# Attention and MoE in one kernel: eight more dummy matmuls in the head, and a kv product moved across a slab boundary

## The chip, the core and the metric

The kernel runs on one core of a Trainium2 chip. The core has five engines that run side by side and wait for each other by semaphores: PE (TensorE, matrix products into the eight banks of PSUM), DVE (VectorE), ACT (ScalarE), POOL (GpSimd) and SP (SyncE, which here only issues DMAs). The metric is the device time of one execution in microseconds (us). Three timed runs of the kernel before gave 280.95, 281.73 and 280.97 us; the median is 280.97 us.

## The reference

Eight batches of linear attention (8 heads, 576 positions, head size 64) feed a two-layer network with a swish that has one beta for each hidden unit. In short:

```python
q_s = softmax(q, axis=-1)                      # over the 64 of a head
k_s = softmax(k, axis=2)                       # over the 576 positions
kv  = einsum('bhsd,bhse->bhde', k_s, v)        # 64 x 64 for each head
x   = einsum('bhsd,bhde->bhse', q_s, kv)       # to (4608, 512)
h   = x @ w_in                                 # (4608, 2048)
g   = h * sigmoid(beta * h)
out = g @ w_out                                # (4608, 512), f32
```

## The kernel before, in words

**Slabs.** The 4608 rows are nine slabs of 512. Slab b (0 to 7) holds the first 512 positions of batch b; slab 8 holds the last 64 positions of all eight. For each slab PE runs two passes. Pass 1 (`pass1_mm`, line 638) makes 16 hidden tiles f of 128 units, each from four products over m (the four head pairs, 128 columns each), `WIN` by `XT`; after the fourth, ACT applies Silu from the PSUM bank into `GT[:, f]` (L646). Pass 2 (`pass2_group`, L727) multiplies `GT` by `WOUT` into four row groups u, each over 16 f; a copy (`o2_evac`, L700) takes each from its bank to `O2S`, and `store` writes it out. The two passes are 64 products of 512 columns each, 0.216 us apart.

**Attention.** For a batch, `exp_q` and `exp_kc` on ACT make the exponentials EQ and EK, `norm_main` on DVE and POOL divides EQ by its row sums, `cast_v` turns V into bf16 with a column of ones behind it. `kv_prods` multiplies EK by V on PE, `kv_evac` divides by the last column on DVE (reciprocal RC, L442, and product KVC, L444). `out_prods` multiplies the transposed EQ (`QT`) by KVC, and `out_evac` (L456) copies the results from PSUM to `XT`: odd head pairs on ACT, even ones on DVE. `kv_half` and `out_half` do two of the four pairs.

**Head.** Batch 0 has its own order, written out by hand (L603 to L634): long f32 dummy products first, then for each head pair four transposes of EQ (`t_steps`), a kv product (`kv_tiles`, 18 products of 65 columns), an out product (`out_now`), and between them four dummies `warm(1, bank)`, one bf16 product of zeros with 512 columns each, read by nobody. Slab 0's pass 1 follows.

**From slab 0 to slab 1.** During slab 0's pass 2, a list `todo` (L754) places batch 1's attention at counted products (`tick`): transposes at 104 and 109, the first kv half at 115, the first out half at 122, then `evacs` at 124.5 (row group u0 by DVE out of bank 3, u1 by ACT out of bank 4, then a dummy activation that brings Silu's table back), and the second kv half at 127, one product before the pass ends. After it come the copy of u2 (bank 5, ACT) and slab 1's opening tiles: for a set of f, all products of m = 0, then all of m = 1 and so on (`by_m`, L655), so that the first rows need only the first XT pairs. `FIRST = (16, 5)` says how many tiles: 16 in slab 0, 5 in slab 1. Between them lie the second out half (banks 7 and 0) and the copy of u3 (bank 6, DVE).

**Banks.** `hbank` (L652) gives pass 1's tile its PSUM bank from a table: slab 1's f0 to f7 take banks 1, 3, 2, 4, 5, 6, 0, 7, and f8 and on take 2, 0, 1 in turn. A product that starts a tile waits until the engine that last read its bank is done.

**What sets the order.** Each engine runs its instructions in the order in which `add` (L57) was called for it. `Program.plan` turns the declared reads, writes and banks into semaphore waits; nothing is reordered. DMAs are issued by SP in the order of the calls as well.

Of the kernel before, what the change touches and what calls it, by code (L numbers as in the profile page):

```python
# [163 lines left out]
def bass_efficient_attn_shen__then__act_swish_beta_kernel(  # L164
# [12 lines left out]
    with ExitStack() as es:  # L177
# [113 lines left out]
        for hp in range(NHP):  # L291
            eng = ACTE if hp % 2 else SP
# [39 lines left out]
        def norm_main(b, hp0, n, eng=DVE):  # L332
            i = b % 2
            a = bass.AP(EQ[i], hp0 * 512, [[2048, 128], [64, 8 * n], [1, 64]])
            s_ = bass.AP(QS[i], hp0 * 8, [[32, 128], [1, 8 * n]])
            v_ = bass.AP(QI[i], hp0 * 8, [[32, 128], [1, 8 * n]])
            vb = bass.AP(QI[i], hp0 * 8, [[32, 128], [1, 8 * n], [0, 64]])
            ks = [("eq", i, hp) for hp in range(hp0, hp0 + n)]
            add(DVE, lambda e: e.tensor_reduce(s_, a, AX.X, ALU.add), r=ks, w=[("qs", i, hp0)])  # L339
            add(DVE, lambda e: e.reciprocal(v_, s_), r=[("qs", i, hp0)], w=[("qi", i, hp0)])  # L340
            add(eng, lambda e: e.tensor_tensor(a, a, vb, ALU.mult), r=ks + [("qi", i, hp0)],  # L341
                w=ks)
# [113 lines left out]
        def out_evac(b, bks, hps=range(NHP)):  # L456
            i = b % 2
            for hp in hps:
                eng, bk = (ACTE if hp % 2 else DVE), bks[hp]
                add(eng, lambda e, eng=eng, bk=bk, hp=hp: (  # L460
                    e.copy if eng == ACTE else e.tensor_copy)(XT[i][:, hp, :], PS[bk][:, :]),
                    r=[("ps", bk)], w=[("xt", i, hp)], bank=[bk])
# [19 lines left out]
        def kv_half(b, bks, a):  # L482
            kv_prods(b, bks, (a,))
            kv_evac(b, bks, (a,))

        def out_half(b, bks, a):
            out_prods(b, bks, (a,))
            out_evac(b, bks, (a, a + 1))
# [53 lines left out]
        def go(steps):  # L542
            for s in steps:
                s()
# [67 lines left out]
        turn_beta()  # L612
        norm_main(0, 2, 1, POOL)
        norm_main(0, 3, 1, POOL)
        go(t_steps(0, (1,), (4,)))
        kv_tiles(0, 7)
        warm(1, 0)
        cast_v(0, 2)
        cast_v(0, 3)
        for m in range(1, NM):  # L620
            cast_win(0, m, POOL)
        cast_win(1, 0, POOL)
        go(t_steps(0, (2,), (5,)))
        warm(1, 0)
        kv_tiles(1, 1)
        out_now(0, 0, 0, ACTE)
        go(t_steps(0, (3,), (6,)))
        warm(1, 3)
        kv_tiles(2, 7)
        out_now(0, 1, 5, ACTE)  # L630
        cast_win(0, 0, DVE)
        warm(1, 3)
        out_now(0, 2, 0, ACTE)
        kv_tiles(3, 1)  # L634

# [1 line left out]

        def pass1_mm(t, f, m, bk):
            x = XT8 if t == 8 else XT[t % 2]
            rd = [("xt8", 0)] + [("xt8", p_, y) for p_ in range(1, 4) for y in range(2)] if t == 8 else [("xt", t % 2, m)]  # L640
            n = 2 if f < 8 else 4
            l = bass.AP(WIN, m * DFF + 128 * (f // n * n) + f % n, [[NM * DFF, 128], [n, 128]])
            mm(PS[bk][:, :], l, x[:, m, :], m == 0, m == NM - 1,
               r=rd + [("win", f // 4, m)], w=[("ps", bk)], bk=bk)
            if m == NM - 1:
                add(ACTE, lambda e: e.activation(GT[:, f, :], PS[bk][:, :], ACT.Silu,  # L646
                                                 scale=BETA[:, f:f + 1]),
                    r=[("ps", bk), "beta"], w=[("gt", f)], bank=[bk])
# [15 lines left out]
                pass1_mm(t, f, m, bk)  # L664
                tick()

        FIRST = (16, 5)
        at = by_m(0, 0, 4)
        at(0)
        out_now(0, 3, 7, DVE)  # L670
# [74 lines left out]
        for t in range(NSLAB):  # L745
            todo = []
            if t == 0:
                def evacs():
                    o2_evac(0, 0, 3, DVE)
                    o2_evac(0, 1, 4, ACTE)  # L750
                    add(ACTE, lambda e: e.activation(DUMMY[:, 2:3], WARM[:, 0:1], ACT.Silu),
                        r=["warm"], w=["dummy"])

                todo = [(104, lambda: go(t_steps(1, (0, 1), (1,), ACTE))),  # L754
                        (104.1, lambda: cast_v(1, 0, ACTE)),
                        (109, lambda: go(t_steps(1, (2, 3), (2,), ACTE))),
                        (109.1, lambda: (scale_wout(14, 2), exp_kc(1, 2), exp_kc(1, 3))),
                        (115, lambda: kv_half(1, (7, 0), 0)),
                        (122, lambda: out_half(1, (1, 2), 0)), (124.5, evacs),
                        (127, lambda: kv_half(1, (7, 0), 2))]  # L760
            elif t == 1:
                todo = [(103, lambda: (kv_prods(2, (1, 2), (0, 2)), kv_evac(2, (1, 2)))),
                        (118, lambda: block(2))]
            elif t < 7:
                todo = [(104, lambda: block(t + 1))]
            todo = sorted(todo, key=lambda x: -x[0])
            slot = [0]

            def tick():
                slot[0] += 1  # L770
                while todo and todo[-1][0] <= slot[0]:
                    todo.pop()[1]()

            if 2 <= t < 7:
                if t < 5:
                    load(t + 2 if t == 2 else t + 3)
                for hp in (0, 2):
                    norm_main(t + 1, hp, 2)
                    t_dma(t + 1, hp, 2)
                if t in (2, 3, 4, 6):  # L780
                    norm_rem(t // 2 if t != 3 else 0)
                    tr_dma(t // 2 if t != 3 else 0)
                if t == 2:
                    load(5)
            elif t == 1:
                for hp in range(NHP):
                    cast_v(2, hp)
            if t < 2:
                slot[0] = NM * FIRST[t]
            for f in range(FIRST[t] if t < 2 else 0, NF):  # L790
                pass1_tile(t, f, tick)
            if t == 0:
                load(2)
                scale_wout(0)
                scale_wout(4)
                exp_q(1, (0,))
                norm_main(1, 0, 1)
                scale_wout(8)
                exp_q(1, (1, 3, 2))
                norm_main(1, 1, 1, POOL)  # L800
                norm_main(1, 3, 1, POOL)
                norm_main(1, 2, 1)
                exp_kc(1, 0, 2)
                scale_wout(12, 2)
                for hp in range(1, NHP):
                    cast_v(1, hp)
                pass2_group(0, (0, 1, 2, 3), (3, 4, 5, 6), tick)
                while todo:
                    todo.pop()[1]()
                at = by_m(1, 0, FIRST[1])  # L810
                o2_evac(0, 2, 5, ACTE)
                at(0, 0, 3)
                at(1, 0, 3)
                out_half(1, (7, 7, 7, 0), 2)
                o2_evac(0, 3, 6, DVE)
                at(0, 3)
                at(1, 3)
                at(2)
                at(3)
                store(0)  # L820
                load(3)
                load_qrem(0)
                continue
            nb = [t + 2] if t + 2 < B else []
            if t == 1:
                nb = [2, 3]
            late = []
            for b in nb:
                if t == 1 and b == 2:
                    exp_q(2)  # L830
                    for hp in range(2):
                        norm_main(2, hp, 1, POOL)
                    t_dma(2, 0, 2)
                for hp in (0, 2):
                    exp_kc(b, hp, 2)
                if b > 2:
                    late.append(b)
                if b > 3:
                    for hp in range(NHP):
                        cast_v(b, hp)  # L840
            for b in late:
                exp_q(b)
                if b % 2 == 1:
                    exp_qr(b // 2)
                if b == 3:
                    exp_qr(0)
            for u in range(4):
                if (t, u) == (8, 3):
                    last_tile(u, ((0, 384), (384, 512)), (OB[orot[0] % 2], MB[0]))
                    continue  # L850
                pass2_group(t, (u,), (OB[orot[0] % 2],), tick)
                orot[0] += 1
                if t == 1 and u == 0:
                    for hp in range(2, 4):
                        norm_main(2, hp, 1, POOL if hp == 2 else DVE)
                    t_dma(2, 2, 2)
                    for hp in range(NHP):
                        cast_v(3, hp)
            while todo:
                todo.pop()[1]()  # L860
            if t < 8:
                store(t)
# [30 lines left out]
```

## Time and profile before

| what | value |
| --- | --- |
| median of three runs | 280.97 us |
| profiled execution | 281.7 us |
| its span, first to last instruction | 279.9 us |
| busy share PE / DVE / ACT / POOL | 97% / 37% / 60% / 12% |
| chain that ended last, PE's share | 94% |
| slab 0's first product starts at | 16.05 us |
| second kv half of batch 1 on PE | 45.86 us |
| its last inputs are cast by | 44.20 us (EK, ACT), 44.99 us (V, POOL) |

How to read it: the page gives one execution, all times from the first instruction. A group row names the source line, the engine, the operation, what is written from what, the shapes, and how often. Most of PE's rows have L371 or L373, the helper `mm`, so they are told apart by their tiles: `PS<-WARM` is a dummy, `PS<-IDB,EQ` a transpose, `PS<-VB,EK` a kv product, `PS<-QT,KVC` an out product, `PS<-XT,WIN` pass 1 and `PS<-WOUT,GT` pass 2. Busy time counts an instruction until its result is written; a matmul of 512 columns lasts 0.38 us by its row though the next starts 0.216 us after it. PEclk is the share of full TensorE clock that was granted. In brackets stands the engine's idle time before a row and what ended it. Some matmul records are missing from the trace: after kv products a hole of 0.16 us marked "issue" is one of them.

### The profile page before, as it was taken

To read this page: it belongs to the slowest core of one execution; us is meant where nothing else is said; L and a number is where in the kernel's file an instruction comes from. 1 tells how busy PE (TensorE), PEld (TensorE's weight loads), DVE (VectorE), ACT (ScalarE), POOL (GpSimd) and SP (SyncE) were. 2 spreads that over 40 slices of the span, in tenths; PEclk is the share of its full clock that TensorE was granted. 3 is DMA by queue.
4 is the path that set the end of the run, shared out by engine and by line. 5 is a ranking of instruction groups with operands and counts; after the bars stand their busy time and mean duration, and the time that the engine had idled before them with its cause. 6 is when DMAs were issued, how large, how long until landed. Compare 5 with 4: busy or idle time off the path is not lost.

```text
span 279.9 us, 4581 instructions
## 1 busy us (share of the span) xinstructions
PE 270.9 (97%) x1892; PEld 131.8 (47%) x1922; DVE 103.0 (37%) x206; ACT 166.6 (60%) x240; POOL 33.2 (12%) x50
## 2 busy tenths in 40 slices
PE   7799999999999999999999999999999999999995
PEld 2545454454445454545454544444444444444443
DVE  3663695007590157305640463035603300110012
ACT  4657777789767835794479537853751276017500
POOL 2630041306100305030002100000000000000000
PEclk9689999999999999999999999999999999999999
DMA  7999999997279998970499134001600120011022
GB/s 226 387 388 401 388 390 376 360 384 119 42 239 389 204 374 229 387 171 2 144 356 235 40 129 96 2 4 75 169 0 2 49 101 2 0 74 76 2 75 75
DMA packets 42173, 50.12 MB, mean 179 GB/s; under 512 B 21028, under 2 KB 29476, under 8 KB 41000
## 3 DMA queue, kind: packets, MB, share of 16 engines
q1 hardware_dynamic: 41168, 48.77, 54.3%
q10 hardware_dynamic: 984, 1.06, 1.2%
q8 instruction: 15, 0.25, 0.4%
q14 instruction: 6, 0.05, 0.0%
HBM read 36.71 MB, written 9.44 MB: 165 GB/s over the span
## 4 chain that ended last, share of the span: by engine, by line
PE 94%; DMA 2%; issue 1%; ACTq 0%; ACT 0%; DVE 0%
PE PS L373 93%; DMA QF<-in_q_dram 2%; PE PS L371 1%; ACTq L299 0%; ACT EK L323 0%; ACT VB L358 0%; DVE O2S L722 0%; ACT EQ L315 0%; ACTq L147 0%
## 5 line engine op out<-in xcount | busy, mean ns | idle before, releaser
L646 ACT ACTIVATE GT<-PS,BETA 128x512 bf16<-128x512 f32 x144 | 96.9, 689 | 61.3 <-PE PS L373 61.3
L373 PE MATMUL PS<-WOUT,GT 128*128 128x512 bf16 (+2 forms) x573 | 125.0, 373 | 1.8 <-issue 1.3
L373 PE MATMUL PS<-XT,WIN 128*128 128x512 bf16 x566 | 125.8, 379 | 0.7 <-issue 0.2
L373 PEld LDWEIGHTS PS<-XT,WIN 128*128 128x128 bf16 x576 | 60.4, 106 | 63.6 <-issue 0.5
L373 PEld LDWEIGHTS PS<-WOUT,GT 128*128 128x128 bf16 x592 | 56.5, 98 | 65.8 <-issue 1.1
L701 DVE COPY O2S<-PS 128x512 f32<-128x512 f32 x33 | 22.7, 688 | 124.1 <-PE PS L373 124.1
L358 POOL CAST VB<-VF 128x576 bf16<-128x576 f32 x29 | 20.8, 718 | 84.8 <-DMA VF<-in_v_dram 83.2
L339 DVE TENSOR_REDUCE QS<-EQ 128x8 f32<-128x512 bf16 (+1 forms) x22 | 20.1, 913 | 19.6 <-ACT EQ L315 19.6
L460 ACT CAST XT<-PS 128x512 bf16<-128x512 f32 x14 | 7.6, 589 | 23.9 <-PE PS L373 23.9
L315 ACT ACTIVATE EQ<-QF 128x512 bf16<-128x512 f32 x32 | 17.7, 617 | 3.5 <-DMA QF<-in_q_dram 3.5
L323 ACT ACTIVATE EK<-KF 128x1152 bf16<-128x1152 f32 (+1 forms) x19 | 18.4, 1005 | 1.7 <-DMA KF<-in_k_dram 1.6
L341 DVE TENSOR_TENSOR EQ<-EQ,QI 128x1024 bf16<-128x1024 bf16 (+1 forms) x14 | 16.3, 1164 | 0.5
L460 DVE CAST XT<-PS 128x512 bf16<-128x512 f32 x14 | 9.1, 688 | 13.4 <-PE PS L373 13.4
L341 POOL TENSOR_TENSOR EQ<-EQ,QI 128x512 bf16<-128x512 bf16 x8 | 8.3, 1043 | 35.4 <-DVE QI L340 35.0
L373 PEld LDWEIGHTS PS<-VB,EK 64*64 64x64 bf16 x576 | 7.4, 112 | 5.3 <-issue 2.5
L373 PE MATMUL PS<-VB,EK 64*64 64x65 bf16 x576 | 8.9, 200 | 1.0 <-ACT VB L358 0.6
L373 PE MATMUL PS<-QT,KVC 64*64 64x512 bf16 x64 | 6.9, 405 | 0.0
L646 ACT ACT_TABLE_LOAD x5 | 6.4, 1283 | 0.1
L373 PE MATMUL PS<-XT 128*128 128x512 f32 x6 | 5.0, 998 | 1.5 <-DVE XT L226 1.5
L340 DVE RECIPROCAL QI<-QS 128x8 f32<-128x8 f32 (+1 forms) x22 | 5.0, 226 | 0.8
L323 ACT ACT_TABLE_LOAD x4 | 5.1, 1283 | 0.1
L444 DVE TENSOR_TENSOR KVC<-PS,RC 128x128 bf16<-128x128 f32 (+1 forms) x16 | 4.4, 275 | 0.6
(51 smaller groups left out, 66.6 us busy)
## 6 DMA issues: line engine op xcount, KB each, us to landing
out_dram<-O2S SPq DMA_DIRECT2D x8, 1024.0 KB, 4.5
QF<-in_q_dram SPq DMA_DIRECT2D x30, 256.0 KB, 5.7
KF<-in_k_dram SPq DMA_DIRECT2D x6, 1152.0 KB, 8.0
VF<-in_v_dram SPq DMA_DIRECT2D x6, 1152.0 KB, 10.9
KF<-in_k_dram SPq DMA_DIRECT2D x8, 288.0 KB, 8.3
VF<-in_v_dram SPq DMA_DIRECT2D x8, 288.0 KB, 8.6
WST<-in_moe_w_in_dram SPq DMA_DIRECT2D x8, 256.0 KB, 7.6
O2S<-in_moe_w_in_dram SPq DMA_DIRECT2D x4, 512.0 KB, 11.8
```

The source lines that it names most:

```text
L315: add(ACTE, lambda e, o=o, a=a: e.activation(o, a, ACT.Exp), r=[("qf", i, hp, x) for x in ((2, 3) if hp % 2 else (hp // 2,))], w=[("eq", i ...
L323: add(ACTE, lambda e: e.activation(o, a, ACT.Exp), r=[("kf", i, h) for h in range(hp, hp + n)], w=[("ekc", i, h) for h in range(hp, hp + n)])
L339: add(DVE, lambda e: e.tensor_reduce(s_, a, AX.X, ALU.add), r=ks, w=[("qs", i, hp0)])
L340: add(DVE, lambda e: e.reciprocal(v_, s_), r=[("qs", i, hp0)], w=[("qi", i, hp0)])
L341: add(eng, lambda e: e.tensor_tensor(a, a, vb, ALU.mult), r=ks + [("qi", i, hp0)], w=ks)
L358: add(eng, lambda e: (e.copy if eng == ACTE else e.tensor_copy)(o, a), r=[("vf", i, hp), ("vone", i)], w=[("vb", i, hp, h) for h in ((0, 1 ...
L371: add(PE, lambda e: e.transpose(o, l, r_), r=r, w=w, bank=[bk])
L373: add(PE, lambda e: e.matmul(o, l, r_, start=start, stop=stop, tile_position=tp), r=r, w=w, bank=[bk])
L444: add(DVE, lambda e, o=o, p_=p_, vb=vb: e.tensor_tensor(o, p_, vb, ALU.mult), r=[("ps", bk)] + [("rc", i, hp) for hp in hps], w=[("kvc", k ...
L460: add(eng, lambda e, eng=eng, bk=bk, hp=hp: (e.copy if eng == ACTE else e.tensor_copy)(XT[i][:, hp, :], PS[bk][:, :]), r=[("ps", bk)], w=[ ...
L646: add(ACTE, lambda e: e.activation(GT[:, f, :], PS[bk][:, :], ACT.Silu, scale=BETA[:, f:f + 1]), r=[("ps", bk), "beta"], w=[("gt", f)], ba ...
L701: add(eng, lambda e: (e.copy if eng == ACTE else e.tensor_copy)(O2S[t % 2][:, u, :], PS[bk][:, :]), r=[("ps", bk)], w=[("o2", t % 2, u)], ...
```

## The change

Five edits. (1) The head gets eight more bf16 dummies (the change's own summary counts nine): two new ones ahead of pair 1's transposes, and 3, 2, 2, 3 where there was one each. (2) Batch 1's second kv half leaves the list at 127 and stands in slab 1, behind two products of the opening tiles; the copy of u3 (bank 6) follows it directly and no longer the second out half. (3) Slab 1 opens with six tiles, and is split behind two tiles and not three. (4) In batch 1, pairs 2 and 3 swap engines for their XT copies: pair 2 on ACT, pair 3 on DVE. (5) Slab 8's products name all eight copies into XT8 as their inputs. In the order of instructions the kernel has eight matmuls more and no other instruction more or less; on DVE the copy of u3 comes ahead of an XT copy; SP's order of DMAs is the same.

```diff
@@ out_evac
-                eng, bk = (ACTE if hp % 2 else DVE), bks[hp]
+                eng, bk = (ACTE if (hp % 2) != (b == 1 and hp > 1) else DVE), bks[hp]
@@ the head
         norm_main(0, 3, 1, POOL)
+        warm(2, 0)
         go(t_steps(0, (1,), (4,)))
         kv_tiles(0, 7)
-        warm(1, 0)
+        warm(3, 0)
         cast_v(0, 2)
...
         go(t_steps(0, (2,), (5,)))
-        warm(1, 0)
+        warm(2, 0)
         kv_tiles(1, 1)
         out_now(0, 0, 0, ACTE)
         go(t_steps(0, (3,), (6,)))
-        warm(1, 3)
+        warm(2, 3)
         kv_tiles(2, 7)
         out_now(0, 1, 5, ACTE)
         cast_win(0, 0, DVE)
-        warm(1, 3)
+        warm(3, 3)
         out_now(0, 2, 0, ACTE)
         kv_tiles(3, 1)
@@ pass1_mm
-            rd = [("xt8", 0)] + [("xt8", p_, y) for p_ in range(1, 4) for y in range(2)] if t == 8 else [("xt", t % 2, m)]
+            rd = ([("xt8", p_, y) for p_ in range(4) for y in range(2)] if t == 8
+                  else [("xt", t % 2, m)])
@@ opening tiles
-        FIRST = (16, 5)
+        FIRST = (16, 6)
@@ todo of slab 0
-                        (122, lambda: out_half(1, (1, 2), 0)), (124.5, evacs),
-                        (127, lambda: kv_half(1, (7, 0), 2))]
+                        (122, lambda: out_half(1, (1, 2), 0)), (124.5, evacs)]
@@ the end of slab 0
                 o2_evac(0, 2, 5, ACTE)
-                at(0, 0, 3)
-                at(1, 0, 3)
+                at(0, 0, 2)
+                kv_half(1, (7, 0), 2)
+                o2_evac(0, 3, 6, DVE)
+                at(0, 2)
+                at(1, 0, 2)
                 out_half(1, (7, 7, 7, 0), 2)
-                o2_evac(0, 3, 6, DVE)
-                at(0, 3)
-                at(1, 3)
+                at(1, 2)
                 at(2)
                 at(3)
```

## The prediction, made before the changed kernel ran

> **What bounds the kernel now.** I read first the page's busy shares and clock row, then the clock by windows of the head, then PE's timeline of the head, then the timeline of all engines around the step from slab 0 to slab 1, and last the place where slab 1 reuses its banks.
>
> ```profile
> PE 270.9 (97%) x1892; PEld 131.8 (47%) x1922; DVE 103.0 (37%) x206; ACT 166.6 (60%) x240; POOL 33.2 (12%) x50
> ...
> PEclk9689999999999999999999999999999999999999
> ```
>
> PE has work 97% of the span, and the chain that ended last is PE for 94%. Only the third and second slices of the clock row (7 to 21 us) are short of full clock. So the end moves by what PE loses or gains, and by nothing else that isn't in PE's way. The windows view (columns: stretch, busy time and count by engine, granted clock, DMA share, GB/s):
>
> ```profile
> 5.85:9.26 3.41, 2.31 (x18) 1.49 (x16) 3.21 (x9) 1.42 (x3) 1.23 (x2) 1.00 1.00 360
> 9.26:12.68 3.42, 2.78 (x48) 1.70 (x45) 1.72 (x6) 3.16 (x6) 2.56 (x3) 0.50 1.04 388
> 12.68:16.10 3.42, 3.06 (x56) 1.80 (x50) 1.86 (x6) 1.27 (x4) 2.33 (x4) 0.50 1.05 398
> ```
>
> The clock is whole until 9.26, half until 16.10, whole after. PE was busy 68%, 81% and 90% of the three stretches. PE's timeline of the head (start, duration, what):
>
> ```profile
> 9.05 0.45 PE L371 MATMUL PS<-IDB,EQ 128*128 128x128 bf16 x4
> 10.13 0.70 PE L373 MATMUL PS<-VB,EK 64*64 64x65 bf16 x18 [0.64 <-ACT VB L358]
> 10.77 0.61 PE L373 MATMUL PS<-WARM 128*128 128x512 bf16 x1
> 11.17 0.63 PE L371 MATMUL PS<-IDB,EQ 128*128 128x128 bf16 x4
> 11.60 0.63 PE L373 MATMUL PS<-WARM 128*128 128x512 bf16 x1
> ...
> 16.05 1.04 PE L373 MATMUL PS<-XT,WIN 128*128 128x512 bf16 x4
> ```
>
> One idle stretch of 0.64 us lies in the middle window; slab 0's first product starts at 16.05. From there on PE has no idle time but a few 0.05 and 0.16 us, and the 0.16 us follow kv products where one matmul record is missing. The step to slab 1, all engines:
>
> ```profile
> 43.52 0.68 ACT L323 ACTIVATE EK<-KF 128x576 bf16<-128x576 f32 x1 [0.80 <-DMA KF<-in_k_dram]
> 44.32 0.67 POOL L358 CAST VB<-VF 128x576 bf16<-128x576 f32 x1 [0.85 <-DMA VF<-in_v_dram]
> ...
> 44.68 1.25 PE L373 MATMUL PS<-WOUT,GT 128*128 128x512 bf16 x5
> ...
> 45.86 0.48 PE L373 MATMUL PS<-VB,EK 64*64 64x65 bf16 x36
> 45.92 1.28 ACT L751 ACT_TABLE_LOAD   x1
> ...
> 46.50 1.46 PE L373 MATMUL PS<-XT,WIN 128*128 128x512 bf16 x6 [0.16 <-issue]
> ...
> 46.92 0.23 DVE L444 TENSOR_TENSOR KVC<-PS,RC 128x64 bf16<-128x64 f32 x1
> ...
> 47.33 0.57 ACT L701 COPY O2S<-PS 128x512 f32<-128x512 f32 x1
> ...
> 48.94 0.68 DVE L701 COPY O2S<-PS 128x512 f32<-128x512 f32 x1
> ```
>
> The last two rows empty banks 5 and 6. Nobody waits for them now. And the bank that slab 1's tenth tile (f9, bank 0) gets back from tile f6's Silu:
>
> ```profile
> 54.04 1.30 ACT L646 ACTIVATE GT<-PS,BETA 128x512 bf16<-128x512 f32 x2
> ...
> 54.81 0.15 PEld L373 LDWEIGHTS PS<-XT,WIN 128*128 128x128 bf16 x2 [0.41 <-ACT GT L646]
> ```
>
> f9 starts at 54.82, 0.10 later than its turn: this wait is already at its edge.
>
> [...] in the trace six take 1.46, (1.46 - 0.38)/5 = 0.216, and four cold transposes take 11.60 - 11.17 = 0.43, 0.107 each. [...] here the ACT copy of 47.33 indeed stands behind the table load of 45.92. [...] the trace has 1.28 and the next activation at once, so I use 1.28.
>
> **The change, part by part.**
>
> *Dummies* (there are eight more, 2+2+1+1+2). The first two stand before head pair 1's transposes at 9.05, and the clock falls at 9.26 with or without them, since the idle parts of that window (6.46 to 7.11, 7.49 to 7.94) lie ahead of them. One warm, one cold, then cold transposes: done at 9.05 + 0.22 + 0.43 + 0.43 = 10.1. The kv product waits for VB until 10.13 anyway, so they cost 0.07 at most; without that cover 0.65. But they fill the idle 0.64, so the window 9.26 to 12.68 is dense, and by the 81% / 90% above I take the clock to rise at 12.68 and not at 16.10. Work from there, in cold microseconds: 16.05 - 10.20 = 5.85 that was there, plus two dummies 0.85, plus four 1.71, is 8.41. Until 12.68, 2.48 of it is done; the other 5.93 takes 2.97 warm, so slab 0 would start at 15.65. Adding each step's fixed lead (a matmul to a kv product 0.31 warm, against half of 0.56) gives 15.85. DVE's cast of WIN (15.09 to 15.82 now, behind the third KVC) moves up likewise and ends beside it. I take 15.75: **gain 0.30**, bounds 0.2 and 0.4. With the clock up no earlier they would cost 0.07 + 6 x 0.43 = 2.6, all in PE's way.
>
> *Second kv half moved into slab 1.* Its 36 products, two reciprocals and two multiplies are the same work, no DMA moves. PE's order is now 6 WOUT, 2 XT, kv, 6 XT, QT; it was 5, kv, 1 + 6, QT. VB's last cast ends at 44.99 and kv starts at 45.86, so it waits for nothing today: moving gains nothing, and its new place alone costs nothing in PE work. On DVE kv's four instructions now stand just ahead of the copy that empties bank 6.
>
> *Six opening tiles, 24 products ahead of tile 6 where there were 20.* Same count in all, but the first row needs banks 5 and 6 earlier. From 44.68: six WOUT to 45.98; f0 and f1 at 45.98 and 46.20 (bank 3 is empty at 45.39 + 0.68 = 46.07: just in time); kv at 46.51; 0.42 later f2 at 46.93, f3 47.15, f4 due 47.37, f5 due 47.58. f4 needs bank 5: ACT copy ends 47.33 + 0.57 = 47.90, so f4 starts 47.94. f5 needs bank 6: DVE's kv part ends in the old place at 47.15 for a kv start of 45.86, so at 47.80 for 46.51; the copy overlaps it by 0.09 and takes 0.68, ending at 48.39; f5 starts at 48.43. **Loss 0.85**, bounds 0.55 (if DVE is quicker and bank 5 alone holds) and 1.0. Behind the waiting matmul stands all of PE. Both copies hang on PE's own out products (44.34), so an earlier head doesn't shorten this.
>
> *The tenth tile.* Seven Silus run back to back from the last row: from its start 50.19 to the end of f6's at 54.76 is 4.57. With five tiles f9 is due 5 x 0.216 + 16 x 0.216 = 4.54 after that start, with six 6 x 0.216 + 12 x 0.216 = 3.89. ACT is no faster, so f9 waits 4.63 - 3.89 = 0.74 where it waited 0.10: **loss 0.64**, bounds 0.5 and 0.7, zero only if ACT caught up, which a 0.57 pace against 0.216 excludes.
>
> *XT copies on swapped engines.* Pair 2 goes from DVE (0.69) to ACT (0.59), pair 3 the other way, DVE behind bank 6's copy. Four products lie between QT and pair 2's row (0.86), ten before pair 3's: hidden, cost 0; without them 0.1. *The other read list of slab 8* adds a wait on copies done some 20 us before: 0.
>
> Sum against the profiled execution: 281.7 - 0.30 + 0.85 + 0.64 = 282.9. That execution (span 279.9) lies 0.75 above two of the three timed runs (280.95, 280.97; the third is 281.73). I estimate that the windows' phase makes this: where a window opens after the idle 0.64, the old head also gets its clock a window earlier and slab 0 starts up to 0.85 sooner. With the change that idle is gone; as the rise falls between 11.7 and 13.4, slab 0 starts at 15.3 to 16.1, on average somewhat ahead of 15.75. So **282.6**, 0.6% over the median.
>
> **Rivals.** *The clock never falls* (0.11). The two dummies at 9.05 carry the window. Then kv runs at 10.13, and by the data (VB of the last pair 13.52, WIN's cast) slab 0 starts near 14.65, a gain of 1.4: 281.7 - 1.4 + 0.85 + 0.64 = 281.8, not slower by what this measurement can tell (0.3%, 0.84 us). It decides whether the clock row shows any half clock after 9.26. [...] Against it: these dummies add no busy time ahead of 9.26. Also EK and VB of the last pair come from DMA, which is full (share 1.04), so ACT could not empty bank 5 before 47.2. *Only one of the bank waits costs* (0.15): if the Silus' pace follows PE, or the first wait lets ACT draw level: 282.0. Against: both are counted from PE's own starts, one after the other. *The clock falls again in slab 1* (0.08): 0.85 and 0.74 us of idle lie within two windows; one at half clock costs half of 3.41: 284.3. For: 81% was not enough to raise it. Against: these windows would be 75 to 85% full of 512-column products, and nothing shows that this lowers it. *Faster all the same* (0.04): something in the head that I don't see.
>
> **How the numbers follow.** Forecast 0.62 at 282.6, itself 282.1 to 283.2 by the bounds. Range 281.5 to 283.4: from the lower rivals to the forecast's upper bounds, leaving out the fallen clock and the fast cases. Slower by over 0.3% (above 281.8): 0.62 + 0.13 of the single wait + 0.08 + a third of the first rival, 0.86; same 0.10; faster 0.04.
>
> **What would show it.** Half clock from about 9.3 for one window only; slab 0's first product near 15.75; PE waiting 0.6 us for an ACT copy of O2S and then 0.3 for a DVE copy near 47.5; a wait of 0.7 us on GT at f9 some 4.6 after the last opening row. I am wrong if the clock row shows no cold window or two, or if PE has no idle time between 46 and 56.

## The result, and the profile after

| | before | with the change |
| --- | --- | --- |
| median, us (4 runs each) | 281.22 (280.95 to 281.73) | 283.15 (282.93 to 283.86) |
| ratio, 95% interval | 1 | 1.0071 (1.0046 to 1.0096) |
| profiled execution / its span | 281.7 / 279.9 | 283.33 / 281.5 |

The change makes the kernel slower, by 0.7%; the forecast was 282.6 us, 0.6% over the median it knew. The clock row on the page of the changed kernel:

```profile
PEclk9799999999999999999999999999999999999999
```

The clock is better than before (second slice 7 in place of 6, third 9 in place of 8), and still the span is 1.6 us longer. PE's busy times, 270.9 before and 274.9 now, can't be set against each other: before's page has 1892 matmuls for 1922 weight loads, so 30 records are missing there, and the change's has 1930 of each. The head by windows of the clock (stretch, busy by engine, granted clock, DMA share, GB/s):

```profile
6.21:9.62 3.41, 2.28 (x15) 1.48 (x15) 3.27 (x9) 1.89 (x5) 1.59 (x2) 1.00 1.03 384
9.62:13.04 3.42, 3.42 (x32) 1.94 (x30) 1.17 (x5) 2.40 (x4) 2.41 (x4) 0.50 1.04 395
13.04:16.45 3.41, 3.41 (x72) 1.76 (x71) 1.70 (x7) 1.30 (x3) 2.36 (x4) 1.00 1.05 384
```

One cold window in place of two, and PE without a gap from 9.62 on, as forecast. But slab 0's first product starts at 16.29, not at 15.75. PE there, and at the step to slab 1:

```profile
16.29 1.04 PE L373 MATMUL PS<-XT,WIN 128*128 128x512 bf16 x4
...
47.16 0.61 PE L373 MATMUL PS<-XT,WIN 128*128 128x512 bf16 x2
48.19 1.32 PE L373 MATMUL PS<-XT,WIN 128*128 128x512 bf16 x4 [0.42 <-ACT O2S L703]
...
49.79 6.22 PE L373 MATMUL PS<-XT,WIN 128*128 128x512 bf16 x28
56.58 0.62 PE L373 MATMUL PS<-XT,WIN 128*128 128x512 bf16 x2 [0.58 <-ACT GT L648]
```

ACT at the same place, and DVE:

```profile
47.57 0.57 ACT L703 COPY O2S<-PS 128x512 f32<-128x512 f32 x1
...
52.37 5.99 ACT L648 ACTIVATE GT<-PS,BETA 128x512 bf16<-128x512 f32 x10 [1.90 <-PE PS L373]
```

```profile
47.96 0.68 DVE L703 COPY O2S<-PS 128x512 f32<-128x512 f32 x1
```

PE now has two waits at the step that before did not have, and one that has grown: f4 starts at 48.19, just after ACT's copy of bank 5 (47.57 + 0.57 = 48.14); f5 at 48.69, after DVE's copy of bank 6 (48.64); f9 at 56.58, behind seven Silus. Idle time in brackets begins when the last matmul's result is written, so it is shorter than the loss. Counted from start to start, f3 to f5 take 1.300 where two turns are 0.432, so 0.868 is lost, and f8's last product to f9 takes 0.957, so 0.741 is lost where before lost 0.098.

A ledger for all runs follows from two rows of ACT's timeline, each against before. Slab 0's first Silu (19.51 us before) tells what the head cost ("head"); the time from there to slab 2's first Silu (77.94 before) tells what the stretch between them cost ("step"). Both are of one profiled execution, the medians of all timed ones; the ratios are those of the means, with 95% intervals.

| run | timed median (runs), ratio to before | head | step |
| --- | --- | --- | --- |
| the change | 283.15 (4), 1.0071 | +0.24 | +1.52 |
| e1 dummies only | 281.93 (22), 1.0033 (1.0016 to 1.0049) | +2.03 | +0.02 |
| e2 order only | 282.35 (14), 1.0038 (1.0024 to 1.0052) | -0.56 | +1.53 |
| e3 two dummies | 280.94 (14), 0.9993 (0.9979 to 1.0007) | -0.11 | +0.29 |
| e4 tenth tile's bank | 282.97 (6), 1.0060 (1.0036 to 1.0083) | -1.17 | +1.84 |
| e5 copy of u2 first | 283.34 (4), 1.0080 (1.0048 to 1.0111) | +0.64 | +1.53 |
| e6 copy of u3 first | 283.92 (4), 1.0095 (1.0073 to 1.0117) | -0.07 | +1.30 |
| e8 all three | 283.29 (4), 1.0069 (1.0044 to 1.0094) | +1.34 | +0.38 |
| e9 five tiles | 282.62 (10), 1.0045 (1.0025 to 1.0065) | +0.08 | +0.69 |
| e14 copies not swapped | 284.17 (4), 1.0102 (1.0079 to 1.0126) | +0.49 | +1.53 |
| e11 gap dummies | 280.63 (22), 0.9981 (0.9971 to 0.9991) | -1.37 | +1.22 |
| e12 no dummies | 281.30 (14), 1.0003 (0.9988 to 1.0018) | -0.91 | +0.53 |
| e13 gap, moved, five | 280.38 (6), 0.9969 (0.9957 to 0.9981) | -1.85 | +0.21 |

Before's own median was 281.28 beside e1 to e4 (43 runs), 281.11 beside e5, e6, e8 and e11 (27) and 281.43 beside the others (23). The head of one profile is one draw: the clock fell at 8.44 us in e8's profile and at 9.62 in the change's, and ACT's fourth exponential, behind the last of the first loads, began between 7.84 (the change) and 9.00 (e1). The step repeats to 0.01 where it consists of the same waits on engines alone (1.52 and 1.53 in four runs).

The medians mix executions whose clock fell for a different number of windows. The record has the mean granted clock of every execution. One window of 3.41 us at half clock takes 0.006 off the mean of a span of 280 us, and the recorded values stand in groups: 0.998 to 1.000, 0.992 to 0.994, 0.986 to 0.988, and 0.982. I read them as no, one, two and three cold windows; the profiles agree (the change has one at 0.994, e1 two at 0.988, e11 none at 0.999). The mean time, us (executions), by this count:

| kernel | no cold window | one | two |
| --- | --- | --- | --- |
| before, beside all experiments | 280.94 (6) | 281.04 (55) | 281.64 (32) |
| e1 dummies only | 280.88 (5) | 282.06 (12) | 283.48 (5) |
| e2 order only | 281.81 (1) | 282.24 (9) | 282.94 (4) |
| the change | | 283.27 (4) | |
| e6 | | 283.21 (2) | 284.28 (2) |
| e8 | | 282.68 (2) | 283.54 (2) |
| e14 | | 283.47 (2) | 284.62 (2) |
| e3 two dummies | 280.69 (3) | 280.94 (9) | 281.90 (2) |
| e12 no dummies | | 280.56 (3) | 281.46 (9) |
| e11 gap dummies | 280.67 (22) | | |
| e13 | 280.40 (6) | | |

Two more executions of e12 had three (282.26); e4, e5 and e9 are not listed. An edit can itself change the number of cold windows, so a column is no clean experiment; but it separates what a median mixes.

### The profile page after: what moved, and what is told of

It reads as the page before. It is cut to its first block, busy times and chain, and to the rows that moved or that the text cites. A ratio compares the mean times of both kernels' runs of the same rounds, so it can differ in the third digit from the quotient of the medians.

```text
span 281.5 us, 4627 instructions
## 1 busy us (share of the span) xinstructions
PE 274.9 (98%) x1930; PEld 131.8 (47%) x1930; DVE 103.2 (37%) x206; ACT 166.3 (59%) x240; POOL 33.1 (12%) x50
## 4 chain that ended last, share of the span: by engine, by line
PE 94%; DMA 2%; ACT 1%; ACTq 1%; DVE 1%; issue 0%
PE PS L373 93%; DMA BT<-in_moe_beta_dram 2%; ACT GT L648 1%; PE PS L371 1%; ACTq L299 1%; DVE O2S L703 0%; DVE KVC L444 0%; DVE O2S L724 0%; DVE RC L442 0%
## 5 line engine op out<-in xcount | busy, mean ns | idle before, releaser
L373 PE MATMUL PS<-WOUT,GT 128*128 128x512 bf16 (+2 forms) x592 | 127.7, 374 | 0.0
L373 PEld LDWEIGHTS PS<-VB,EK 64*64 64x64 bf16 x576 | 6.7, 108 | 4.5 <-issue 3.0
L373 PE MATMUL PS<-VB,EK 64*64 64x65 bf16 x576 | 8.1, 195 | 0.0
L373 PE MATMUL PS<-QT,KVC 64*64 64x512 bf16 x64 | 6.2, 384 | 0.0
```

The costliest lines, as they stand in the source:

```text
L373: add(PE, lambda e: e.matmul(o, l, r_, start=start, stop=stop, tile_position=tp), r=r, w=w, bank=[bk])
```

## The experiments

### Which part costs: e1 and e2

e1 is the kernel before with the change's head (12 short dummies in place of 4), e2 the changed kernel with the head of before:

```diff
 # e1, against before            # e2, against the change: the reverse
+        warm(2, 0)   # ahead of pair 1's transposes
-        warm(1, 0) / warm(1, 0) / warm(1, 3) / warm(1, 3)
+        warm(3, 0) / warm(2, 0) / warm(2, 3) / warm(3, 3)
```

> The kernel before with the eight dummies and nothing else of the change. Theory (the two bank waits make the loss, the dummies pay for themselves): slab 0's first product at 15.7 to 16.4, one cold window of 3.41 us in place of two, PE without a wait at 46 to 57; 281.0 to 281.5 us, no difference from before. Rival (the dummies are the loss, eight matmuls in PE's way): 282.5 to 283.2 us.

> The changed kernel with the head of before (four dummies). Theory: both bank waits are there, 0.87 and 0.74 us, where before had 0.10: 281.2 + 1.51 = 282.7 us, slab 0's first product at 16.05 or earlier. Rival (the dummies are the loss): 281.2 us.

Measured by the medians: 0.65 us from the dummies and 1.07 from the order (0.9 and 1.1 by the means), and 1.0033 x 1.0038 is the change's 1.0071. The theory was right about the order and wrong about the dummies: they do not pay for themselves. The rival that they are the whole loss is out as well. The table says where it goes. With one cold window e1 is 1.0 us above before, e2 1.2 and the change 2.2, so the two parts add up; with two, e1 is 1.8 above. What the dummies buy is fewer cold windows, and too few: 1.00 on average in e1, 1.28 in before. e1's profile shows a case with two, first PE, then the two clock windows:

```profile
10.82 0.70 PE L373 MATMUL PS<-VB,EK 64*64 64x65 bf16 x18 [0.68 <-ACT VB L358]
```

```profile
9.49:12.90 3.41, 2.73 (x28) 1.56 (x27) 1.57 (x5) 3.17 (x7) 2.33 (x3) 0.50 0.99 362
12.90:16.32 3.42, 3.42 (x33) 1.51 (x30) 1.24 (x4) 1.10 (x2) 1.89 (x3) 0.50 1.04 391
```

The last q load of batch 0 came late (ACT's exponential of it at 9.00, 8.31 in before's profile), so V was cast late, the gap ahead of the first kv product opened behind the dummies, and the clock stayed down for two windows. Then the seven dummies that run in the cold, where before had three, are 0.43 us each in PE's way ((1.46 - 0.61)/2, from the three at 11.45 in e1's profile and the single one at 10.77 in before's). In e2's profile the step is 1.53, the change's 1.52. That its times are only 1.1 to 1.3 us up, in the columns too, may be before giving back part of an early head (below); no run isolates that, and it stays open.

### The two bank waits: e5, e6, e8

```diff
 # e5: the dummy activation, and with it the table load, behind ACT's copy of u2
 # e6: DVE's copy of u3 ahead of the kv half
+                o2_evac(0, 3, 6, DVE)
                 kv_half(1, (7, 0), 2)
-                o2_evac(0, 3, 6, DVE)
 # e8: e5, e6 and e4 together
```

> The changed kernel with ACT's copy of u2 (bank 5) ahead of the dummy activation and its table load. Theory (f5's wait for bank 6 stands right behind f4's for bank 5 and is as long as both): bank 5 is free before f4's turn, f5 now waits the whole 0.87 us alone, and PE loses the same between the out product and slab 1's first Silu: no change in the step, 283.1 us. Rival (the table load ahead of the copy is the cause): 0.58 us less, 282.6 us.

> The changed kernel with DVE's copy of u3 (bank 6) ahead of the four instructions of the second kv half. Theory: f5's wait goes, f4's wait for ACT's copy stays (0.58 us): PE loses 0.29 us less than with the change, 282.85 us. Rival (bank 6 is the whole wait): 0.87 us less, 282.3 us.

> The changed kernel with both copies moved ahead and f8 to f10 in banks 2, 1, 0. Theory: no wait of PE is left between 46 and 57 us, 0.87 + 0.74 us less, and what is left over before is the head's dummies alone: 281.5 to 281.9 us, as the dummies alone gave. Rival (the order itself costs, by the second kv half or the swapped XT copies): 282.3 us or more.

PE in e5, then in e6:

```profile
49.09 0.82 PE L373 MATMUL PS<-XT,WIN 128*128 128x512 bf16 x3 [0.70 <-DVE O2S L703]
```

```profile
47.88 1.04 PE L373 MATMUL PS<-XT,WIN 128*128 128x512 bf16 x4 [0.42 <-ACT O2S L703]
```

In e5 the first wait is gone and the second, now for DVE alone, is as long as both were: step 1.53, unchanged. In e6 ACT's wait is left: step 1.30, 0.23 less (0.29 expected). In e8 neither is there and the step falls to 0.38. Of these 1.14 the banks of e4 (below) make 0.30, and the rest is the 0.87. So each wait is real, they overlap, and only both moves together take the whole of it away. The medians of four runs do not show it, and the expectations for e6 and e8 missed (283.92 and 283.29 us). Part of that is the draw: two of e6's and two of e8's four executions had two cold windows, none of the change's had. With one, e8 is 0.6 us below the change and e6 0.06, of two executions each. That e8 gains 0.6 there and not 1.1 stays open.

### The tenth tile: e4 and e9

```diff
-        HFIRST = (..., (1, 3, 2, 4, 5, 6, 0, 7))
+        HFIRST = (..., (1, 3, 2, 4, 5, 6, 0, 7, 2, 1, 0))   # e4
-        FIRST = (16, 6)
+        FIRST = (16, 5)                                     # e9
```

> The changed kernel with slab 1's tiles f8, f9 and f10 in banks 2, 1, 0 and not 2, 0, 1: f9 takes the bank of f0, whose Silu is the first to end. Theory: f9's wait of 0.74 us goes and none follows: 283.15 - 0.74 = 282.4 us. Rival (the wait moves on: ACT is behind by its backlog, so another tile waits as long): 283.1 us.

> The changed kernel with five opening tiles (f0 to f4) and all else as changed. Theory: f5 leaves the opening, so bank 6 is not waited for and f9 waits 0.1 us as before; f4's wait for bank 5 (0.58 us) stays. Between slab 0's last Silu and slab 1's first full-pace Silu PE loses 0.6 us in place of 1.5: 282.2 us. Rival (the moved kv half is the loss, whatever the tiles): 283.1 us.

With other banks the wait moves on, as the rival had it, though not in full. Weight loads in e8, which has the same banks:

```profile
57.96 0.58 PEld L373 LDWEIGHTS PS<-XT,WIN 128*128 128x128 bf16 x4 [0.49 <-ACT GT L648]
59.12 0.80 PEld L373 LDWEIGHTS PS<-XT,WIN 128*128 128x128 bf16 x5 [0.57 <-ACT GT L648]
```

From start to start PE loses 0.18 and 0.26 at these two products, 0.43 in e4, in place of 0.74: a backlog of ACT is not cured by dealing its banks in another order. Five tiles cure it. PE in e9:

```profile
48.03 0.82 PE L373 MATMUL PS<-XT,WIN 128*128 128x512 bf16 x3 [0.42 <-ACT O2S L703]
...
49.13 9.24 PE L373 MATMUL PS<-XT,WIN 128*128 128x512 bf16 x41
```

Of the waits on banks f4's alone is left (0.58 from start to start), then 41 products in one run; step 0.69 for an expected 0.6. So the sixth tile, and not the moved kv half, is most of the loss. What is left comes with the new order: before opened f3 and f4 only behind the second out product, from 48.23 on, when bank 5 had been empty since 47.90; the change opens all its tiles ahead of it. In e13 (below), which has this order and an earlier copy of bank 5, no such wait is left.

e4's profile holds a second lesson: its clock never fell (1.0 on the mean). Its two windows ahead of 11.43:

```profile
4.60:8.02 3.42, 1.62 (x7) 0.43 (x5) 2.61 (x7) 1.71 (x4) 0.08 (x1) 1.00 0.94 312
8.02:11.43 3.41, 3.16 (x40) 2.41 (x41) 2.40 (x8) 3.38 (x6) 3.05 (x3) 1.00 1.04 401
```

Slab 0 started at 14.88, and f4's wait grew to 1.24 (start to start 1.459) from the 0.87 of both waits in the change: ACT comes to its copies behind the exponential of a k load that lands no earlier (43.91), so a third of the head's gain of 1.17 was spent there.

### The swapped copies: e14

> The changed kernel with the XT copies of pairs 2 and 3 on the engines of before (2 on DVE, 3 on ACT). Theory: both copies end before their rows' turn on either engine, so slab 1's step loses 1.5 us as with the change; 283.1 us. Rival (the swap saves or costs): 0.1 us either way in the step.

The swap undone, the step is 1.53: no cost and no gain there, as expected. The median is higher than the change's by 1.0 with four runs each and overlapping intervals. Two of e14's four executions had two cold windows, none of the change's; those with one stand at 283.47 against 283.27.

### The head: e3, e11, e12

```diff
 # e3, against before             # e11: all three      # e12: none of before's four
+        warm(3, 0)               # e11, ahead of pair 0's transposes
+        warm(2, 0)               # e11, ahead of beta's
+        warm(2, 0)               # e3 and e11, ahead of pair 1's
```

> The kernel before with only the two dummies ahead of head pair 1's transposes. They lie where PE waits for V anyway (0.64 us) and make that clock window dense. Theory ([...] cost 0.1 or less): one cold window, slab 0's first product at 14.8 to 15.3, and about 0.9 us less than before: 280.1 to 280.6 us. Rival 1 (the gap is not what keeps the clock down): two cold windows, 281.2 us. Rival 2 (slab 0 starts earlier, but DMA-fed steps at 38 to 45 us give it back as waits of PE): 280.8 to 281.2 us.

> The kernel before without its four short dummies. Theory ([...] dummies are work in PE's way where the clock is down): the head has 1.7 us less cold work, but its windows are less full and the clock may come back only when slab 0's own products fill a window; the two about cancel, 281.0 to 281.8 us, with the profile showing half clock under slab 0's first products. Rival (dummies are nothing but cost): 279.6 to 280.2 us.

> The kernel before with seven more dummies, all in idle stretches of PE: three ahead of pair 0's transposes (idle 6.46 to 7.11), two ahead of beta's (7.49 to 7.94), two ahead of pair 1's. Theory (the clock falls because the window that ends at 8 to 11 us has too little matmul work in it; one run kept its clock all through): the clock does not fall, slab 0's first product at 14.3 to 14.9, 280.2 to 280.6 us. Rival 1 (the clock falls whatever fills the gaps): 281.2 us or more. Rival 2 (it stays, but DMA-fed steps at 38 to 45 us give the time back): 280.9 to 281.2 us.

e3 missed: no gain clear of noise. In its profile the clock fell all the same, and V's late cast reopened the gap (0.73 us). Only 2 of its 14 executions had two cold windows, 32 of before's 93, so it may help; the interval does not settle it. e12 came as the theory had it: the same time as with four dummies, with more cold windows (11 of 14 executions had two or three), but 0.5 and 0.2 us below before where both have one or two. PE in e12, cold under slab 0's first products (1.69 us for four; 1.04 when warm):

```profile
14.49 1.69 PE L373 MATMUL PS<-XT,WIN 128*128 128x512 bf16 x4
```

e11 kept the clock: it is whole in the profile's windows from 5.97 to 16.21 and 0.999 on the mean, with slab 0 at 14.68, and all 22 executions stand at 0.998 or more, where before had 6 of 93. The gain in the median is 0.48 us. The profiled execution, at 281.50 the longest of the 22, shows how the rest can go: of 1.37 us gained 1.22 were given back, most of it in one place, rival 2's. PE in e11:

```profile
45.71 0.47 PE L373 MATMUL PS<-VB,EK 64*64 64x65 bf16 x34 [0.65 <-POOL VB L358]
```

The second kv half of batch 1 stands 0.86 us (start to start) until POOL has cast a V that DMA did not deliver sooner. Its cast began at 44.99 here, at 44.32 in before's profile and at 43.80 in e13's, so the size of this loss is a draw as well.

### A version that beats both: e13

e11's dummies, the kv half behind slab 1's first two products, all five tiles (before's number) opened ahead of the second out product, one product of m = 1 there, and ACT's copy of u2 ahead of the table load.

> The kernel before with the seven dummies in PE's idle stretches, the second kv half moved behind slab 1's first two products as in the change, five opening tiles, and ACT's copy of u2 ahead of the table load. Theory: the clock does not fall, slab 0 starts near 14.7; PE comes to the kv half 0.65 us later than with the gap dummies alone, so that its wait for V shrinks from 0.86 to about 0.2 us, and no bank is waited for: 0.6 us less than the gap dummies alone, 280.0 us. Rival (the time goes into the next wait, bank 5 behind ACT's late EK): 280.6 us.

280.38 us, 0.9969 (0.9957 to 0.9981) of before, and 1.0% under the change by the medians. PE in e13:

```profile
44.84 0.48 PE L373 MATMUL PS<-VB,EK 64*64 64x65 bf16 x36
45.26 1.04 PE L373 MATMUL PS<-XT,WIN 128*128 128x512 bf16 x4
...
46.57 10.66 PE L373 MATMUL PS<-XT,WIN 128*128 128x512 bf16 x48
```

No wait is left around the boundary; the step is 0.21 in place of e11's 1.22. Part of that is luck of this profile, whose last V cast ended at 44.47 and not at 45.66 as in e11's. Against e11 the median is 0.25 better, for an expected 0.6, and the intervals overlap. That the moved kv half pays with an early head is likely, not shown, and the moved copy of u2 was not tried apart from it.

## Why the prediction was right, point by point

- **f4 and f5, loss 0.85:** 0.868 measured in the change's profile, and shown by e5, e6 and e8 to be the two copies it named.
- **f9, loss 0.64:** 0.741 - 0.098 = 0.643. The bound "ACT is no faster" held; e4 and e9 show that ACT's backlog is the cause.
- **Moved kv half, swapped copies, slab 8's list at 0:** e9, e13 and e14 agree for the first two, as far as PE's own work goes; that DVE's kv part ahead of bank 6's copy costs is in the term above. The list was not tried alone; slab 8 shows no wait.
- **Dummies, gain 0.30: wrong.** In the profile the head lost 0.24. Of the 0.54 between, 0.18 is the window's later edge (13.04 for 12.68, at half speed), 0.10 had been taken off the 15.85 that the working gave, and the rest is mainly fixed lead counted too low: a kv with an out product took 0.53 warm (13.307 to 13.837), and half of the cold pair before (12.160 to 13.032) is 0.44. Over many executions it is worse: e1 lost 0.65. The failing sentence is "But they fill the idle 0.64, so the window 9.26 to 12.68 is dense": it took V's arrival and the window's edge from one execution. Of 58 executions of the eight kernels with these dummies 11 had no cold window, 33 one and 14 two. And the gain was set against an execution with two, while 55 of before's 93 had only one, where the dummies had little to save.
- **The windows' phase:** that the old head is quicker where it gets its clock a window earlier was right. With one cold window before is 0.60 us below its mean with two (up to 0.85 estimated).
- **The sum:** 282.9 against 283.33 for the profiled execution; 282.6 against 283.15 for the median. The miss in the profile is the head term, 0.54, of which 0.13 came back behind slab 2. In the median the head term missed by about 0.95, and that the sum was only 0.55 off is luck: the working began 0.48 above before's median of 281.22 (0.3 of it taken off again for the phase), and of the 1.49 for the order e2's median shows 1.07.
- **Rivals:** the clock that never falls occurs (11 of 58, e4's profile among them), but it is not the usual case, and with it f4's wait grows as the sentence on bank 5 ("not before 47.2") said: it started at 47.60. The single bank wait is refuted by the profile, by e6 and e9. The clock did not fall again in slab 1: no slice there is below 9.

## What to carry to other kernels

Before more tiles are opened at once, count two things: when the bank of each extra tile is emptied by the engine that holds it, which runs in order (ACT's copy of u2 stood behind a table load of 1.28 us here), and how long the evacuating engine takes for the whole burst, since the backlog came due at a bank used again: f9 lost 0.741 us here. Put dummies only where the trace shows PE idle, and judge them over several executions: e11's seven, in idle stretches of PE, kept the clock in all 22, while e1's eight left 1.00 cold windows on average for 1.28 and were otherwise plain work, 0.43 us each where the clock was half. Before a median of four is believed, see how many cold windows each execution had. And when one stretch is made faster, look at the next DMA-fed step: e11's profile gave back 1.22 of 1.37 us, most of it (0.86) in the wait for V.

## What the runs showed of the hardware

In the change's profile the clock was half for 3.41 us (9.62 to 13.04), in before's for 6.83 (9.26 to 16.09), two windows of that length. PE's busy time did not tell which window was the last cold one. Two windows of e8, in both of which PE was busy without a gap:

```profile
8.44:11.85 3.41, 3.41 (x33) 2.14 (x33) 2.00 (x7) 3.12 (x6) 3.12 (x4) 0.50 1.04 403
11.85:15.26 3.41, 3.41 (x33) 1.86 (x32) 0.82 (x3) 1.17 (x2) 1.95 (x4) 0.50 1.00 363
```

Behind the first the clock stayed at half; behind the second it was whole (three dummies at 16.23 take 0.82, where three in the cold at 11.12 take 1.46). In before, half clock followed on 2.78 busy of 3.42 (9.26 to 12.68) and the whole clock on 3.06 of 3.42 (12.68 to 16.10, with one dummy's record missing); in e1 half clock followed on 2.73 of 3.41 (9.49 to 12.90); in the change the whole clock on 3.42 of 3.42. So to expect the rise from a busy share between 81% and 90% was an estimate from one execution, and e8's first window contradicts it.

Nor did busy time tell when the clock fell. Windows at whole clock with 2.31 of 3.41 busy (before, 5.85 to 9.26), 2.28 (the change, 6.21 to 9.62), 2.36 (e1, 6.08 to 9.49) and 1.80 of 3.42 (e8, 5.02 to 8.44) had half clock behind them; e4's with 1.62 of 3.42 (4.60 to 8.02) had not, nor had e11's with 3.10 of 3.41 (5.97 to 9.38). PE's work in these windows is of different kinds: in e8's first one, beta's eight small f32 transposes run until 9.17. Which kinds hold or raise the clock, and how much of them, no run isolates.

The clock's edges also lie elsewhere in each execution: it fell at 8.44 us in e8's profile, at 9.26 in before's, at 9.49 in e1's and at 9.62 in the change's, and the first loads landed up to 1.2 us apart (ACT's fourth exponential at 7.84 to 9.00). One cold window more moves the mean by 0.6 us in before and by 1.4 in e1. That is not the whole spread: before's executions with one still lie between 280.16 and 281.68, and no run isolates what makes that.
